# First block's MLP in whole fp32 products, weights split into two parts later, and the second block's attention spread over it

## Chip, cores and metric

One core of one Trainium2 chip runs the kernel once. The metric is the device time of that execution in microseconds, here called us.

## What is computed

The reference chains three layers over 4 x 768 = 3072 tokens of width 384:

```python
# 1. linear attention, 8 heads of 48, a gate f per step and channel
f = 1 / (1 + exp(-f_logit))
for t in range(S):
    state = f[:, :, t, :, None] * state + k[:, :, t] (x) v[:, :, t]
    y[:, :, t] = q[:, :, t] @ state
# 2. MLP, 384 -> 2048 -> 384
h = x @ w_in
g = h * clip(h + 3, 0, 6) / 6
x = g @ w_out
# 3. eight experts, 384 -> 1024 -> 384, one expert for a token
e = argmax(x @ w_gate)
out = prob[e] * sigmoid(x @ w_output_gate)[e] * (relu(x @ w1[e]) @ w2[e])
```

## The kernel before

The tokens go in 8 blocks of 384 (`NB`, `TB`). For each block there are four attention units (`attention`, a pair of heads each, `pr` 0 to 3), then the MLP (`mlp`), then the choice of an expert (`choose`, `route`). After the last block the experts run one after the other.

An attention unit gives VectorE (DVE in the profile) two scans, four products, two masks and a few small sums; ScalarE (ACT) its gates and copies; TensorE (PE) a transpose `pk`, and the products `pa`, `pkv` and `py`, all in plain fp32. Its result `py` is copied out as two parts, an upper one in the reduced format fp32r (by ACT) and a lower one, the rest (by DVE, `L301`). Both parts stand in the tile `xx`. Unit 3 writes them to `yx`, and six DMAs on SyncE's queue (SP, `L305`) then move them to their rows of `xx`, which the MLP waits for.

The MLP goes over 16 slices `f` of 128 hidden columns. In each slice it makes `ph` from three tiles of `w_in` and 384 tokens ("up"), applies `relu6`, and two slices later (`LAG`) adds the slice's part to three accumulators ("down"). Two buffers hold `ph`, so that slice f+2 can begin only when `relu6` has read slice f. Each of the six products of a slice is made of three fp32r products (`mm3`, and `L323` to `L325`): upper times upper, upper times lower, lower times upper. Weights therefore stand in four tiles, `wih`, `wil`, `woh`, `wol`.

The first MLP's weights arrive as raw 64-bit words. `split64` loads 512 columns (`raw`, two buffers, so that a load waits until the one before the last has been read), joins them to fp32 with three instructions of DVE (`L138`, `L140`, `L144`) and one of ACT (`L143`), and splits them with one of ACT (`L145`, upper part) and one of DVE (`L146`, lower part). There are 24 such parts; 7 of them are asked for between the attention units of block 0, the others two for each slice of block 0's MLP.

`UNITS` gives the slices of the MLP at which the attention units of later blocks are written: unit 0 of a block goes two blocks ahead at slice 11, the others at slices 0, 5 and 9 of the block ahead. Unit 0 of block 1 stands ahead of block 0's MLP. In block 0 eight pairs of fill writes (`fill`, `L479`, `L481`, to `xs_d` in DRAM) follow the last weight load on SP.

The order on each engine is made by a scheduler with a timeline of its own when the program is built. Every engine then works through its list strictly in order. The line numbers are those of the profile.

Of the kernel before, what the change touches and what calls it, by code (L numbers as in the profile page):

```python
# [838 lines left out]
```

## Time and profile before

| | |
|---|---|
| time, three runs | 868.16, 870.57, 870.67 us (median 870.57) |
| the profiled execution | 870.31 us, of which the profile's span is 868.6 us |
| busy, of the span | PE 808.3 us (93%), DVE 528.4 us (61%), ACT 398.1 us (46%) |
| PE's clock | 0.963 of full speed, mean over the span |

The profile divides the span into stretches and tells for each engine how long it was busy. PE's granted clock is 1.00 at 2.4 GHz and 0.50 at 1.2 GHz. A matmul's record is longer than its share of the stream, since matmuls overlap: the step from one start to the next tells what it costs. The same holds for DVE.

### The profile page before, as it was taken

How to read it: one execution, taken by the hardware profiler on the slowest of the kernel's cores; microseconds unless marked ns; L12 is line 12 of the kernel's file. 1: busy time of each engine (PE TensorE's matmuls, PEld its weight loads, DVE VectorE, ACT ScalarE, POOL GpSimd, SP SyncE). 2: the span in 40 equal slices, each digit the busy share in tenths (PEclk: the TensorE clock that was granted, in tenths of full speed). 3: DMA queues.
4: the chain of work that ended last, by engine and by line, in shares of the span. 5: the costliest groups of instructions: out<-in, count | busy, mean ns of one | idle time of the engine just before them, and what ended most of it. 6: DMA issues, size and time to landing. Idle time of an engine off the chain costs nothing.

```text
span 868.6 us, 14585 instructions
## 1 busy us (share of the span) xinstructions
PE 808.3 (93%) x5530; PEld 748.6 (86%) x5530; DVE 528.4 (61%) x1122; ACT 398.1 (46%) x848; POOL 61.1 (7%) x103
## 2 busy tenths in 40 slices
PE   7458998999998999999999999999999999999994
PEld 3338998998998998998899899899998999999994
DVE  6999975669555578653668744563465354465441
ACT  4556664446434456533446433453253253354321
POOL 2000000100000010010010010010100101101111
PEclk9558999999999999999999999999999999999998
DMA  6565495113012022111111100050345055246510
GB/s 190 177 186 154 153 288 159 39 57 105 9 62 73 17 70 80 42 61 43 48 62 58 40 29 10 20 167 20 119 126 189 25 181 169 88 149 200 168 53 28
DMA packets 42411, 85.01 MB, mean 98 GB/s; under 512 B 5953, under 2 KB 29794, under 8 KB 42332
## 3 DMA queue, kind: packets, MB, share of 16 engines
q1 hardware_dynamic: 39052, 74.50, 28.5%
q0 software_dynamic: 3280, 9.49, 3.0%
q8 instruction: 45, 0.74, 0.4%
q14 instruction: 34, 0.28, 0.1%
HBM read 65.77 MB, written 16.26 MB: 94 GB/s over the span
## 4 chain that ended last, share of the span: by engine, by line
PE 46%; DVE 5%; DMA 4%; ACT 2%; issue 2%; SPq 0%; POOL 0%; POOLq 0%; DVEq 0%; ACTq 0%
PE ph L310 7%; PE ph L312 7%; PE ph L311 7%; PE yacc L311 4%; PE yacc L312 3%; PE acc L323 3%; PE acc L324 3%; PE acc L325 3%; PE yacc L310 3%; DMA raw<-in_w 3%; PE py L591 1%; PE py L291 1%; PE pa L253 1%; PE px L553 1%; DVE w1l L124 1%
## 5 line engine op out<-in xcount | busy, mean ns | idle before, releaser
L310 PE MATMUL ph<-xx,wih 128*128 128x384 f32 x384 | 133.7, 348 | 9.5 <-DMA xx<-yx 6.3
L312 PE MATMUL ph<-xx,wil 128*128 128x384 f32 x384 | 132.9, 346 | 0.0
L311 PE MATMUL ph<-xx,wih 128*128 128x384 f32 x384 | 131.9, 343 | 0.0
L347 ACT ACTIVATE gf<-ph,three 128x384 f32<-128x384 f32 x128 | 73.7, 580 | 125.4 <-PE ph L312 123.3
L323 PE MATMUL acc<-woh,gh 128*128 128x384 f32 x384 | 129.4, 337 | 0.7 <-ACT gh L349 0.7
L324 PE MATMUL acc<-wol,gh 128*128 128x384 f32 x384 | 129.8, 338 | 0.0
L325 PE MATMUL acc<-woh,gl 128*128 128x384 f32 x384 | 122.0, 337 | 0.0
L348 DVE SCALAR_TENSOR_TENSOR gf<-gf,ph 128x384 f32<-128x384 f32 x128 | 70.4, 553 | 80.0 <-ACT gf L347 79.3
L354 DVE SCALAR_TENSOR_TENSOR hl<-ph,hh 128x256 fp32r<-128x256 f32 (+7 forms) x72 | 39.0, 543 | 88.9 <-ACT hh L353 84.0
L350 DVE TENSOR_TENSOR gl<-gf,gh 128x384 fp32r<-128x384 f32 x128 | 70.8, 555 | 34.8 <-ACT gh L349 33.6
L349 ACT CAST gh<-gf 128x384 fp32r<-128x384 f32 x128 | 65.3, 512 | 52.2 <-DVE gf L348 50.7
L353 ACT ACTIVATE hh<-ph 128x256 fp32r<-128x256 f32 (+7 forms) x72 | 34.5, 480 | 115.6 <-PE ph L312 110.2
L310 PEld LDWEIGHTS ph<-xx,wih 128*128 128x128 f32 x384 | 74.0, 193 | 13.0 <-DMA xx<-yx 7.2
L312 PEld LDWEIGHTS ph<-xx,wil 128*128 128x128 f32 x384 | 73.9, 192 | 0.9 <-issue 0.5
L311 PE MATMUL yacc<-hl,w2h 128*128 128x256 f32 (+7 forms) x216 | 71.8, 339 | 3.1 <-DVE hl L354 3.1
L311 PEld LDWEIGHTS ph<-xx,wih 128*128 128x128 f32 x384 | 73.9, 192 | 0.3
L323 PEld LDWEIGHTS acc<-woh,gh 128*128 128x128 f32 x384 | 72.1, 188 | 1.5 <-ACT gh L349 1.0
L324 PEld LDWEIGHTS acc<-wol,gh 128*128 128x128 f32 x384 | 72.1, 188 | 1.1 <-issue 0.7
L325 PEld LDWEIGHTS acc<-woh,gl 128*128 128x128 f32 x384 | 71.2, 188 | 0.8 <-issue 0.3
L310 PE MATMUL ph<-xh,w1h 128*128 128x256 f32 (+7 forms) x216 | 71.9, 334 | 0.0
L311 PE MATMUL ph<-xl,w1h 128*128 128x256 f32 (+7 forms) x216 | 71.7, 332 | 0.0
L312 PE MATMUL ph<-xh,w1l 128*128 128x256 f32 (+7 forms) x216 | 71.6, 332 | 0.0
(161 smaller groups left out, 1434.9 us busy)
## 6 DMA issues: line engine op xcount, KB each, us to landing
raw<-in_w SPq DMA_DIRECT2D x23, 512.0 KB, 6.1
raw<-in_w SPq DMA_DIRECT2D x30, 384.0 KB, 3.4
vs<-in_v SPq DMA_DIRECT2D x32, 192.0 KB, 2.5
raw<-in_w_in SPq DMA_DIRECT2D x12, 512.0 KB, 4.0
raw<-in_w_out SPq DMA_DIRECT2D x12, 512.0 KB, 3.5
xt<-in_fl SPq DMA_DIRECT2D x32, 168.0 KB, 3.1
kt<-in_k SPq DMA_DIRECT2D x32, 168.0 KB, 2.4
qt<-in_q SPq DMA_DIRECT2D x32, 168.0 KB, 2.5
```

The source lines that it names most:

```text
L310: nc.tensor.matmul(ps, lhsT=wh, rhs=xh, start=first, stop=False)
L311: nc.tensor.matmul(ps, lhsT=wh, rhs=xl, start=False, stop=False)
L312: nc.tensor.matmul(ps, lhsT=wl, rhs=xh, start=False, stop=last)
L323: nc.tensor.matmul(acc[t], lhsT=gh[:, ts_], rhs=w2h[:, f, :], start=f == 0, stop=False)
L324: nc.tensor.matmul(acc[t], lhsT=gh[:, ts_], rhs=w2l[:, f, :], start=False, stop=False)
L325: nc.tensor.matmul(acc[t], lhsT=gl[:, ts_], rhs=w2h[:, f, :], start=False, stop=f == nf - 1)
L347: nc.scalar.activation(gf, ph, AF.Relu, bias=three)
L348: nc.vector.scalar_tensor_tensor(out=gf, in0=gf, scalar=6.0, in1=ph, op0=ALU.min, op1=ALU.mult)
L349: nc.scalar.copy(gh, gf)
L350: nc.vector.tensor_tensor(out=gl, in0=gf, in1=gh.bitcast(F32), op=ALU.subtract)
L353: return (nc.scalar.activation(gh, ph, AF.Relu).ins, nc.vector.scalar_tensor_tensor(out=gl, in0=ph, scalar=0.0, in1=gh.bitcast(F32), op0=A ...
L354: nc.vector.scalar_tensor_tensor(out=gl, in0=ph, scalar=0.0, in1=gh.bitcast(F32), op0=ALU.max, op1=ALU.subtract).ins)
```

## The change

Block 0's MLP takes whole fp32 weights, whole fp32 activations (`x0`, one plane and not two), and one plain fp32 product in place of three fp32r products. `narrow` only joins the words. The tiles of `w_in` keep 512 columns (12 parts), those of `w_out` get 384 (16 parts and not 12). `halve` makes the two parts of a weight for block 1 and later; it is written at slice 11 of block 0 and at the start, slice 2 and slice 6 of block 1. A lower part takes the place of the whole weight before it (`place`), so that its writing waits until block 0 has read that. `relu6` of block 0 writes whole values, and its upper copy and lower subtraction fall away, as do those of the attention result. The units of block 1 are written at slices 0, 4, 8 and 11 of block 0; those of block 2 at the start and slices 2, 5 and 9 of block 1.

```diff
@@ -126,42 +126,63 @@
     SW = 1024
     loads = []
-    def split64(pool, hi, lo, src):
-
-        raw = work.tile([P, SW // 2, 2], U32, tag="raw", name="raw64")
+    def narrow(pool, t, src):
+
+        n = t.shape[1]
+        raw = work.tile([P, SW // 2, 2], U32, tag="raw", name="raw64")[:, 0:n]
         loads.append(nc.sync.dma_start(out=raw.rearrange("p n t -> p (n t)"), in_=src))
         lw, hw = raw[:, :, 0], raw[:, :, 1]
-        s = pool.tile([P, SW // 2], U32, tag="s64", name="s64", bufs=2)
-        t = s.bitcast(I32)
-        r = pool.tile([P, SW // 2], I32, tag="r64", name="r64")
+        r = pool.tile([P, SW // 2], I32, tag="r64", name="r64")[:, 0:n]
+        s = t.bitcast(U32)
         nc.vector.tensor_scalar(out=s, in0=hw, scalar1=3, scalar2=0x3FFFFFFF, op0=ALU.logical_shift_left,
                                 op1=ALU.bitwise_and)
-        nc.vector.scalar_tensor_tensor(out=t.bitcast(U32), in0=hw, scalar=0xC0000000, in1=s, op0=ALU.bitwise_and,
+        nc.vector.scalar_tensor_tensor(out=s, in0=hw, scalar=0xC0000000, in1=s, op0=ALU.bitwise_and,
                                        op1=ALU.bitwise_or)
         nc.scalar.activation(r, lw, AF.Copy, scale=2.0 ** -29)
-        nc.vector.tensor_tensor(out=t, in0=t, in1=r, op=ALU.add)
-        nc.scalar.copy(hi, t.bitcast(F32))
-        nc.vector.tensor_tensor(out=lo, in0=t.bitcast(F32), in1=hi.bitcast(F32), op=ALU.subtract)
-
-    def first_weights(pool):
-        return [pool.tile(sh, F32R, name=n) for n, sh in (("wih", [P, KD, FF]), ("wil", [P, KD, FF]),
-                                                          ("woh", [P, NF, DM]), ("wol", [P, NF, DM]))]
-
-    def load_first(pool, i, wih, wil, woh, wol):
-
-        wohf, wolf = (t.rearrange("p f d -> p (f d)") for t in (woh, wol))
-
-        def up(kt):
-            sl = slice(i * 512, (i + 1) * 512)
-            split64(pool, wih[:, kt, sl], wil[:, kt, sl], w_in.bitcast(U32)[:, kt, 1024 * i:1024 * (i + 1)])
-
-        def down(j):
-            sl = slice(j * 512, (j + 1) * 512)
-            split64(pool, wohf[:, sl], wolf[:, sl], w_out.bitcast(U32)[:, 1024 * j:1024 * (j + 1)])
-
-        return [partial(up, kt) for kt in range(KD)] + [partial(down, j) for j in range(3 * i, 3 * i + 3)]
+        nc.vector.tensor_tensor(out=t.bitcast(I32), in0=t.bitcast(I32), in1=r, op=ALU.add)
+
+    class FirstWeights:
+
+
+
+        def __init__(self, pool, temp):
+            self.pool, self.temp = pool, temp
+            self.hi = [pool.tile(sh, F32R, name=n) for n, sh in (("wih", [P, NF // 4, KD, 512]), ("woh", [P, NF, DM]))]
+            self.whole, self.lo = ({}, {}), ({}, {})
+
+        def place(self, k, j, dt):
+            return (self.temp if j == (KD * NF // 4, NF)[k] else self.pool).tile([P, (512, DM)[k]], dt, tag=f"{'io'[k]}{j}", name=f"{'io'[k]}{j}")
+
+        def load(self, k, j):
+            t = self.whole[k][j] = self.place(k, j + 1, F32)
+            i, kt = divmod(j, KD)
+            narrow(self.temp, t, w_in.bitcast(U32)[:, kt, 1024 * i:1024 * (i + 1)] if k == 0 else
+                   w_out.bitcast(U32)[:, 2 * DM * j:2 * DM * (j + 1)])
+
+        def halve(self, k, j):
+            t = self.whole[k].pop(j)
+            hi = self.hi[0].rearrange("p i k c -> p (i k) c")[:, j, :] if k == 0 else self.hi[1][:, j, :]
+            self.lo[k][j] = self.place(k, j, F32R)
+            split(hi, self.lo[k][j], t, nc.vector)
+
+        def parts(self, do, i):
+
+            return [partial(do, 0, 3 * i + kt) for kt in range(KD)] + [partial(do, 1, f) for f in range(4 * i, 4 * i + 4)]
+
+        def up(self, kt, f):
+            i, c = f // 4, slice(f % 4 * P, f % 4 * P + P)
+            j = KD * i + kt
+            return (None, self.whole[0][j][:, c]) if j in self.whole[0] else (self.hi[0][:, i, kt, c], self.lo[0][j][:, c])
+
+        def down(self, f):
+            return (None, self.whole[1][f]) if f in self.whole[1] else (self.hi[1][:, f, :], self.lo[1][f])
+
...
-        nc.scalar.copy(yx[:, 0, :], py)
-        freed[1:] = [nc.vector.tensor_tensor(out=yx[:, 1, :], in0=py, in1=yx[:, 0, :].bitcast(F32), op=ALU.subtract)]
+        hl = xx.shape[1]
+        yx = xx[:, :, pr, :] if pr < 3 else at1.tile([P, hl, TB], xx.dtype, tag="yx", name="yx")
+        freed[1:] = [nc.scalar.copy(yx[:, 0, :], py)]
+        if hl == 2:
+            freed[1:] = [nc.vector.tensor_tensor(out=yx[:, 1, :], in0=py, in1=yx[:, 0, :].bitcast(F32),
+                                                 op=ALU.subtract)]
...
         def second(f):
-            gh, gl = gs.pop(f)
+            g, (wh, wl) = gs.pop(f), w.down(f)
             for t in range(3):
                 ts_ = slice(t * P, (t + 1) * P)
-                nc.tensor.matmul(acc[t], lhsT=gh[:, ts_], rhs=w2h[:, f, :], start=f == 0, stop=False)
-                nc.tensor.matmul(acc[t], lhsT=gh[:, ts_], rhs=w2l[:, f, :], start=False, stop=False)
-                nc.tensor.matmul(acc[t], lhsT=gl[:, ts_], rhs=w2h[:, f, :], start=False, stop=f == nf - 1)
+                if wh is None:
+                    nc.tensor.matmul(acc[t], lhsT=g[0][:, ts_], rhs=wl, start=f == 0, stop=f == nf - 1)
+                    continue
+                gh, gl = g
+                nc.tensor.matmul(acc[t], lhsT=gh[:, ts_], rhs=wh, start=f == 0, stop=False)
+                nc.tensor.matmul(acc[t], lhsT=gh[:, ts_], rhs=wl, start=False, stop=False)
+                nc.tensor.matmul(acc[t], lhsT=gl[:, ts_], rhs=wh, start=False, stop=f == nf - 1)
...
+                wh, wl = w.up(kt, f)
+                if wh is None:
+                    nc.tensor.matmul(ph, lhsT=wl, rhs=x[0][:, kt, :], start=kt == 0, stop=kt == KD - 1)
+                else:
+                    mm3(ph, wh, wl, x[0][:, kt, :], x[1][:, kt, :], kt == 0, kt == KD - 1)
+            gs[f] = [pool.tile([P, TB], x[0].dtype, tag=n, name=n, bufs=3) for n in ("gh", "gl")[:len(x)]]
+            act(pool, ph, *gs[f])
...
-    def relu6(pool, ph, gh, gl):
+    def relu6(pool, ph, gh, gl=None):
         gf = pool.tile([P, TB], F32, tag="gf", name="gf")
         nc.scalar.activation(gf, ph, AF.Relu, bias=three)
-        nc.vector.scalar_tensor_tensor(out=gf, in0=gf, scalar=6.0, in1=ph, op0=ALU.min, op1=ALU.mult)
-        nc.scalar.copy(gh, gf)
-        nc.vector.tensor_tensor(out=gl, in0=gf, in1=gh.bitcast(F32), op=ALU.subtract)
+        nc.vector.scalar_tensor_tensor(out=gh if gl is None else gf, in0=gf, scalar=6.0, in1=ph, op0=ALU.min, op1=ALU.mult)
+        if gl is not None:
+            nc.scalar.copy(gh, gf)
+            nc.vector.tensor_tensor(out=gl, in0=gf, in1=gh.bitcast(F32), op=ALU.subtract)
...
-            xts[blk] = blkp.tile([P, 2, KD, TB], F32R, tag="xx", name="xx")
+
+            xts[blk] = blkp.tile([P, 1, KD, TB], F32, tag="xx", name="x0") if blk == 0 else blkp.tile(
+                [P, 2, KD, TB], F32R, tag="xx", name="xx")
         attention(blk, pr, xts[blk])
-    wfirst = first_weights(m1)
+    wfirst = FirstWeights(m1, cv)
     UNITS = (-5, 0, 5, 9)
-    parts = [part for i in range(NF // 4) for part in load_first(cv, i, *wfirst)]
-    for pr, n in enumerate((0, 3, 3, 1)):
+    starts = {(blk - 1, f) if f >= 0 else (blk - 2, f + NF): (blk, pr) for blk in range(3, NB) for pr, f in enumerate(UNITS)}
+    starts.update({(0, f): (1, pr) for pr, f in enumerate((0, 4, 8, 11))})
+    starts.update({(1, f): (2, pr) for pr, f in enumerate((-1, 2, 5, 9))})
+    halves = dict(zip(((0, 11), (1, -1), (1, 2), (1, 6)), range(4)))
+    parts = [part for i in range(NF // 4) for part in wfirst.parts(wfirst.load, i)]
+    for pr, n in enumerate((0, 3, 3, 2)):
         att_unit(0, pr)
         with tc.issue_after(ready[-1]):
             for _ in range(n):
                 parts.pop(0)()
-    for pr in range(4):
-        if UNITS[pr] < -1:
-            att_unit(1, pr)
...
+            for part in wfirst.parts(wfirst.halve, halves[blk, f]) if (blk, f) in halves else ():
+                part()
             if blk == 0 and f >= NF - E:
                 with tc.issue_after(loads[-1].ins):
                     fill(f - NF + E)
-            for pr in range(4):
-                if f == UNITS[pr] and blk + 1 < NB:
-                    att_unit(blk + 1, pr)
-                if f == UNITS[pr] + NF and blk + 2 < NB:
-                    att_unit(blk + 2, pr)
+            if (blk, f) in starts:
+                att_unit(*starts[blk, f])
         between(-1)
         xx = xts.pop(blk)
-        acc = mlp(blkp, xx[:, 0], xx[:, 1], *wfirst, NF, relu6, between)
+        acc = mlp(blkp, [xx[:, i] for i in range(xx.shape[1])], wfirst, NF, relu6, between)
```

The scheduler makes of it the following. On DVE, early in the program (unit 1 of block 0 and the first three weight parts), these rows stand before:

```order
L140 SCALAR_TENSOR_TENSOR s64_325<-raw64_323,s64_325 128x512
L235 SCALAR_TENSOR_TENSOR r0_353<-xt_345,rmax_155 112x384
L144 ISA s64_315<-s64_315,r64_316 128x1024
L238 TENSOR_TENSOR kt_344<-kt_344,r0_353 112x384
L146 TENSOR_TENSOR wil_163<-s64_315,wih_162 128x512
L260 TENSOR_TENSOR at_270<-pa1_272,nmask_100 128x384
L144 ISA s64_325<-s64_325,r64_326 128x1024
L260 TENSOR_TENSOR at_270<-pa0_271,nmask_100 128x384
L138 TENSOR_SCALAR s64_335<-raw64_333 128x512
```

and these now:

```order
L140 SCALAR_TENSOR_TENSOR i2_317<-raw64_318,i2_317 128x512
L256 SCALAR_TENSOR_TENSOR r0_343<-xt_335,rmax_155 112x384
L144 ISA i1_309<-i1_309,r64_312 128x1024
L259 TENSOR_TENSOR kt_334<-kt_334,r0_343 112x384
L144 ISA i2_317<-i2_317,r64_320 128x1024
L138 TENSOR_SCALAR i3_325<-raw64_326 128x512
L124 TENSOR_TENSOR i0_1021<-i1_309,wih_162 128x512
L281 TENSOR_TENSOR at_267<-pa1_269,nmask_100 128x384
L281 TENSOR_TENSOR at_267<-pa0_268,nmask_100 128x384
```

The first reading of the third weight part (`L138`) now stands ahead of the unit's two masks (`L260`, now `L281`); one lower part (`L124`) is made here, and the others wait.

On DVE, up to the first `relu6` of block 0's MLP, these rows stand before:

```order
L260 TENSOR_TENSOR at_567<-pa0_568,nmask_100 128x384
L240 SCALAR_TENSOR_TENSOR kb_668<-rg_665,kt_649 112x384
L235 SCALAR_TENSOR_TENSOR r0_944<-xt_936,rmax_155 112x384
L281 TENSOR_TENSOR st_220<-st_220,pkv_578 112x48
L140 SCALAR_TENSOR_TENSOR s64_788<-raw64_786,s64_788 128x512
L146 TENSOR_TENSOR wol_165<-s64_778,woh_164 128x512
L242 TENSOR_TENSOR qt_934<-qt_934,gg_943 112x384
L237 TENSOR_TENSOR rg_951<-r0_944,gg_943 112x384
L238 TENSOR_TENSOR kt_935<-kt_935,r0_944 112x384
L281 TENSOR_TENSOR st_220<-st_220,pkv_578 112x48
L144 ISA s64_788<-s64_788,r64_789 128x1024
L138 TENSOR_SCALAR s64_824<-raw64_822 128x512
L348 SCALAR_TENSOR_TENSOR gf_623<-gf_623,ph_611 128x384
```

and these now:

```order
L144 ISA o8_666<-o8_666,r64_669 128x768
L302 TENSOR_TENSOR st_218<-st_218,pkv_599 112x48
L254 SCALAR_TENSOR_TENSOR gg_1053<-th_1052,zero_154 112x384
L261 SCALAR_TENSOR_TENSOR kb_923<-rg_920,kt_904 112x384
L256 SCALAR_TENSOR_TENSOR r0_1054<-xt_1046,rmax_155 112x384
L140 SCALAR_TENSOR_TENSOR i7_685<-raw64_686,i7_685 128x512
L138 TENSOR_SCALAR i8_693<-raw64_694 128x512
L258 TENSOR_TENSOR rg_1061<-r0_1054,gg_1053 112x384
L259 TENSOR_TENSOR kt_1045<-kt_1045,r0_1054 112x384
L377 SCALAR_TENSOR_TENSOR gh_537<-gf_538,ph_533 128x384
```

The first `relu6` (`L348`, now `L377`) is the 128th row of DVE before and the 124th now; the scans and products of block 1's units 1 to 3 (`gg`, `r0`, `kb`, `kt`, `rg`) have moved ahead of it.

On PE, at the start of block 0's MLP, these rows stand before (`ph_713` and `ph_750` are slices 1 and 2, `py_587` is block 1's unit 0, `pk_672` its unit 1):

```order
L311 MATMUL ph_713<-xx_166,wih_162 128x384
L312 MATMUL ph_713<-xx_166,wil_163 128x384
L291 MATMUL py_587<-at_567,vs_540 64x128 x2
L294 MATMUL py_587<-qt_537,sbd0_158 64x128 x2
L291 MATMUL py_587<-at_567,vs_540 64x128 x2
L294 MATMUL py_587<-qt_537,sbd0_158 64x128 x2
L291 MATMUL py_587<-at_567,vs_540 64x128 x2
L294 MATMUL py_587<-qt_537,sbd0_158 64x128 x2
L248 MATMUL pk_672<-ident_95,kb_668 128x112 x3
L310 MATMUL ph_750<-xx_166,wih_162 128x384
L311 MATMUL ph_750<-xx_166,wih_162 128x384
L312 MATMUL ph_750<-xx_166,wil_163 128x384
```

and these now (`ph_533`, `ph_623`, `ph_647` are slices 0, 1 and 2, `py_608` is block 1's unit 0, `pk_752` its unit 1, `gh_537` what the first `relu6` writes):

```order
L361 MATMUL ph_533<-x0_164,i3_325 128x384
L361 MATMUL ph_623<-x0_164,i3_325 128x384
L312 MATMUL py_608<-at_588,vs_561 64x128 x4
L315 MATMUL py_608<-qt_558,sbd0_158 64x128 x2
L312 MATMUL py_608<-at_588,vs_561 64x128 x2
L315 MATMUL py_608<-qt_558,sbd0_158 64x128 x2
L269 MATMUL pk_752<-ident_95,kb_748 128x112 x3
L361 MATMUL ph_647<-x0_164,i1_309 128x384
L361 MATMUL ph_647<-x0_164,i2_317 128x384
L361 MATMUL ph_647<-x0_164,i3_325 128x384
L348 MATMUL acc0_530<-o1_405,gh_537 128x384
```

Slice 2 takes the buffer of slice 0 and so waits for the first `relu6`, as it did before; one row (`L361`) now stands where three did (`L310` to `L312`).

## Rows read from the trace of the kernel before

**Rows 1.** Busy by stretch: length, PE, PEld, DVE, ACT, POOL us, PE's clock, DMA.

```profile
40.00:60.00 20.00, 11.02 (x72) 7.71 (x73) 18.72 (x40) 11.77 (x27) 0.00 (x0) 0.50 0.59 179
```

**Rows 2.** Timeline of PE: start us, us, line, op, out<-in, shapes, count, [idle before, releaser].

```profile
65.09 0.66 PE L310 MATMUL ph<-xx,wih 128*128 128x384 f32 x1 [0.75 <-DMA xx<-yx]
75.93 0.67 PE L310 MATMUL ph<-xx,wih 128*128 128x384 f32 x1
```

**Rows 3.** Busy time in block 0 from slice 2 on, and in block 1.

```profile
75.90:135.90 60.00, 59.49 (x439) 55.96 (x440) 54.66 (x113) 36.45 (x78) 0.00 (x0) 0.99 0.70 218
...
145.66:208.50 62.84, 62.84 (x466) 58.91 (x466) 45.67 (x103) 32.96 (x78) 3.51 (x5) 1.00 0.19 55
```

**Rows 4.** Timeline of DVE between the first scan of unit 1 and the first relu6.

```profile
14.85 0.96 DVE L233 TENSOR_TENSOR_SCAN gg<-th,zero 112x384 f32<-112x384 f32 x1
...
60.85 0.67 DVE L144 CUSTOM_DVE_ANT_0 s<-s,r 128x1024 uint16<-128x1024 uint16 x1
61.44 0.56 DVE L301 TENSOR_TENSOR yx<-py,yx 128x384 fp32r<-128x384 f32 x1
61.91 0.95 DVE L235 TENSOR_TENSOR_SCAN r<-xt,rmax 112x384 f32<-112x384 f32 x1
62.77 0.67 DVE L140 SCALAR_TENSOR_TENSOR s<-raw,s 128x512 uint32<-128x512 uint32 x1
63.35 0.56 DVE L242 TENSOR_TENSOR qt<-qt,gg 112x384 f32<-112x384 f32 x1
...
72.83 0.43 DVE L138 TENSOR_SCALAR s<-raw 128x512 uint32<-128x512 uint32 x1
73.16 0.56 DVE L348 SCALAR_TENSOR_TENSOR gf<-gf,ph 128x384 f32<-128x384 f32 x1
```

**Rows 5.** Timeline of SP: the issue of the third weight load.

```profile
19.11 0.37 SPq L132 DMA_DIRECT2D raw<-in_w_in  x1
```

**Rows 6.** Timeline of DVE: two readings of weight words that waited for their load.

```profile
24.36 0.43 DVE L138 TENSOR_SCALAR s<-raw 128x512 uint32<-128x512 uint32 x1 [0.18 <-DMA raw<-in_w_in]
...
50.14 0.43 DVE L138 TENSOR_SCALAR s<-raw 128x512 uint32<-128x512 uint32 x1 [1.17 <-DMA raw<-in_w_in]
```

**Rows 7.** Timeline of PE: a `pk`; two records of one plain fp32 product, twice (`keep_warm`).

```profile
8.76 0.48 PE L248 MATMUL pk<-ident,kb 112*128 112x112 f32 x3 [1.47 <-DVE kb L240]
...
9.07 0.50 PE L69 MATMUL warm<-kb,pad 112*128 112x384 f32 x1
...
9.41 0.49 PE L69 MATMUL warm<-kb,pad 112*128 112x384 f32 x1
...
31.04 0.87 PE L69 MATMUL warm<-kb,pad 112*128 112x384 f32 x1
...
31.71 0.85 PE L69 MATMUL warm<-kb,pad 112*128 112x384 f32 x1
```

**Rows 8.** Timeline of PE: three split products and the next.

```profile
79.09 0.33 PE L310 MATMUL ph<-xx,wih 128*128 128x384 f32 x1
...
79.61 0.33 PE L310 MATMUL ph<-xx,wih 128*128 128x384 f32 x1
```

**Rows 9.** Timeline of PE: unit 0 of block 2, and from block 0 to block 1.

```profile
130.98 0.94 PE L253 MATMUL pa<-qt,kb 48*128 48x128 f32 x12
...
132.33 0.44 PE L325 MATMUL acc<-woh,gl 128*128 128x384 f32 x1
...
135.83 0.66 PE L291 MATMUL py<-at,vs 128*64 128x128 f32 x8
...
137.08 0.87 PE L366 MATMUL px<-ident,row 128*128 128x128 f32 x6
140.40 0.41 PE L310 MATMUL ph<-xx,wih 128*128 128x384 f32 x1 [2.44 <-DMA xx<-yx]
...
145.66 0.44 PE L310 MATMUL ph<-xx,wih 128*128 128x384 f32 x1
```

**Rows 10.** Timeline of SP: the block's six DMAs behind the fill writes.

```profile
114.99 0.43 SPq L479 DMA_DIRECT2D xs_d<-pad  x1
...
134.07 5.61 SPq L305 DMA_DIRECT2D xx<-yx  x6
```

More of the change, by code (lines that the diff above doesn't have):

```diff
@@ L166, in second_weights, with __init__ @@
+    class SecondWeights:
+        def __init__(self, w1h, w1l, w2h, w2l):
+            self.up = lambda kt, f: tuple(w[:, kt, f * P:(f + 1) * P] for w in (w1h, w1l))
+            self.down = lambda f: (w2h[:, f, :], w2l[:, f, :])
     def second_weights(pool):
@@ L297, in attention @@
         in_turn(products)
-        yx = xx[:, :, pr, :] if pr < 3 else at1.tile([P, 2, TB], F32R, tag="yx", name="yx")
-        nc.scalar.copy(yx[:, 0, :], py)
-        freed[1:] = [nc.vector.tensor_tensor(out=yx[:, 1, :], in0=py, in1=yx[:, 0, :].bitcast(F32), op=ALU.subtract)]
+        hl = xx.shape[1]
[4 more added lines that the diff above has]
+                                                 op=ALU.subtract)]
         if pr == 3:
@@ L312, in mm3, with mlp @@
         nc.tensor.matmul(ps, lhsT=wl, rhs=xh, start=False, stop=last)
-    def mlp(pool, xth, xtl, w1h, w1l, w2h, w2l, nf, act, between=None):
+    def mlp(pool, x, w, nf, act, between=None):
         acc = [ps_acc.tile([P, DM], F32, tag=f"acc{t}", name=f"acc{t}") for t in range(3)]
@@ L329, in mlp @@
             ph = ps_h.tile([P, CAP], F32, tag="h", name="ph")[:, 0:TB]
-            fs = slice(f * P, (f + 1) * P)
             for kt in range(KD):
-                mm3(ph, w1h[:, kt, fs], w1l[:, kt, fs], xth[:, kt, :], xtl[:, kt, :], kt == 0, kt == KD - 1)
-            gh = pool.tile([P, TB], F32R, tag="gh", name="gh", bufs=3)
-            gl = pool.tile([P, TB], F32R, tag="gl", name="gl", bufs=3)
-            act(pool, ph, gh, gl)
-            gs[f] = (gh, gl)
+                wh, wl = w.up(kt, f)
[5 more added lines that the diff above has]
+            act(pool, ph, *gs[f])
             if f >= LAG:
@@ L729, in fused @@
             gp = es.enter_context(tc.tile_pool(name="gw", bufs=1))
-            wg1 = first_weights(gp)
-            for i in range(NF // 4):
-                for part in load_first(gp, i, *wg1):
-                    part()
+            wg1 = FirstWeights(gp, gp)
+            for do in (wg1.load, wg1.halve):
+                for i in range(NF // 4):
+                    for part in wg1.parts(do, i):
+                        part()
             with tc.For_i(0, NB, 1) as nb:
@@ L750, in keep @@
                     nc.sync.dma_start(out=x2_d[bass.ds(nb, 1)].rearrange("a p k t -> p (a k) t"), in_=x2)
-                row, oh = choose(gp, mlp(gp, xth, xtl, *wg1, NF, relu6), keep)
+                row, oh = choose(gp, mlp(gp, (xth, xtl), wg1, NF, relu6), keep)
                 gs = gp.tile([P, E, 3, 2], F32, tag="gs", name="gs")
@@ L780, in fused @@
                     nc.sync.dma_start(out=yo, in_=yo_d[bass.ds(nb, 1)].rearrange("a p t d -> p (a t) d"))
-                    acc = mlp(gp, xth, xtl, *w2s, NFE, relu)
+                    acc = mlp(gp, (xth, xtl), SecondWeights(*w2s), NFE, relu)
                     for t in range(3):
```

## The prediction

> **What bounds the kernel now.** I read the table of stretches first. From 40 to 60 us DVE is busy 18.72 of 20 us and PE 11.02, at a granted clock of 0.50 [rows 1]: until block 0's MLP gets going, the kernel waits for DVE. From 75.90 to 135.90 PE is busy 59.49 of 60.00 us, and in block 1, from 145.66 to 208.50, all of 62.84 [rows 3]: from there a microsecond more of PE's work is a microsecond more of time, and any free time of DVE is worth nothing.
>
> The point where the one limit hands over to the other stands in two timelines. PE's slices 0 and 1 begin at 65.09, when `xx` has landed, but slice 2 begins only at 75.93 [rows 2]: it needs the buffer of slice 0, so the first `relu6`, and that stands on DVE at 73.16 behind weight parts and attention [rows 4]. I call this `relu6` the turn. The last place is the step from block 0 to block 1: the last product of block 0 ends at 135.9 (the end of the first stretch of [rows 3]), unit 0 of block 2 has its `py` after it, and block 1's first product comes at 140.40 after 2.44 us of idle waiting for `xx`. Its third slice begins at 145.66 [rows 9]. The six DMAs were issued at 134.07, behind fill writes that had begun at 114.99 [rows 10].
>
> **What a product costs.** A split product is three records and steps 0.52 us (79.09 to 79.61 [rows 8]). A plain fp32 product over 384 columns is two records with 0.34 from start to start (9.07 to 9.41), or 0.67 each later, from 31.04 to 31.71 [rows 7]. At full clock I take 0.667 for the product: 0.147 more than split. The change has fewer records and costs PE more. The 90 products from slice 2 of block 0 on (14 slices up, 16 down, three each) cost 60.0 instead of 46.8 us, +13.2. The six of slices 0 and 1 lie before the turn. The rows are given to 0.01, so the bounds are 0.65 and 0.68 (two steps of 0.34): 58.5 and 61.2.
>
> The Trainium skill speaks against the change more strongly: "FP8 and Floating Point Precision", section "TensorE Precision Notes", gives true FP32 four passes through the array. By four passes at a third of 0.52 each, a product would cost 0.693 us (an estimate from that page and the row above), the 90 products 62.4 us, and the end would come 2.4 us later than I forecast. The step in the trace is near this and I go by the step.
>
> **DVE up to the turn.** From the first scan at 14.85 to the turn at 73.16 [rows 4] DVE passes 58.3 us with 111 rows of its list. In the new list:
> - lower halves of weights (`L146`): 12 go, 2 `L124` come. The neighbours of 512 columns step 0.59 (60.85 to 61.44) and 0.58 (62.77 to 63.35) [rows 4]; ten at 0.6 are -6.0;
> - four lower halves of the attention result (`L301`, 0.47 from 61.44 to 61.91 [rows 4]): -1.9;
> - joining: 14 `L138`, 13 `L140`, 13 `L144` of 512 columns become 16, 15 and 14, of which about half have 384. With 0.33 for `L138` (72.83 to 73.16), 0.6 for the others [rows 4] and 384 in proportion: -0.2;
> - two scans (0.86, 61.91 to 62.77 [rows 4]) and three products at 0.47 of block 1's units come ahead of the turn: +3.1.
>
> The net is -5.0 us of work. Waits come against it. The first reading of the third load now stands two rows after the second part's last step, ahead of the masks. That load was issued at 19.11 [rows 5], its reading in the old order was at 24.36 and had to wait 0.18, and another load cost 1.17 at 50.14 [rows 6]. By my sum DVE gets to the third reading at 21.5, so it waits 2.75 for a landing at 24.3. Behind that `L138` stand the masks of unit 1 and all the rest. I add 1.1 for one more like that of 50.14 and 0.65 for a `w_out` part: 4.5 us of stalls. Before there were 2.6 in all: 1.35 for these two loads and the rest small waits for PE and ACT, for which the longer stand at the load leaves time. Turn: 73.16 - 5.0 + 1.9 = 70.1. With no stalls at all it is 65.6, with 7 us of them 72.6.
>
> Can `x0` be later than that? Before, 3.1 us passed from the end of `L301` (61.44 + 0.56 [rows 4]) to 65.09. The lower half is gone and the list ahead is shorter, so I expect the first product at 58 to 60. Slices 0 and 1 take 4.0 us, or 8.0 at the longer step of [rows 7]: done by 68. If nothing came earlier, it would be 69 to 73. So DVE keeps the turn. The scans and products that moved ahead are also why slice 2 need not wait longer than the `relu6` (before, unit 1's `pk` stood between and waited for its `kb` on DVE, behind the `relu6`): slice 2 begins at 70.5, against 75.93.
>
> **Block 0 from slice 2.** Of PE's 59.49 us [rows 3], 46.8 were products, so 12.7 attention. Unit 0 of block 2 leaves: `pa` and `pkv` from 130.98 to 132.33, 1.35 [rows 9], `pk` 0.31 (8.76 to 9.07 [rows 7]). That leaves 11.0. Last down product: 70.5 + 60.0 + 11.0 = 141.5, 5.6 later. DVE was busy 54.66 us here [rows 3]. It loses 16 lower subtractions of `relu6` (16 at 0.47, 7.5 us) and the rest of 24 `L146`, and gets 26 `L124`, each of which waits until block 0 has read the place that it writes. Going through both new lists row by row with these prices, DVE stays ahead until slice 8 and then waits for PE, never the other way; this cover is some 3 to 6 us.
>
> **The step to block 1.** The last `py` of unit 3 now stands three products before block 0's end (2 us), and its six DMAs come after it, at about 140, when the fills (ended by 134 before, and not moved later) are gone from SP. From `py` to a landed `xx` I take 4 us, 3.1 for the transfer as above and the copies: 1.9 us of wait after the last product, in which `px` runs. Then 18 records up to the third slice at 0.173 (a third of 0.52), 3.1, where before they took 5.26 (140.40 to 145.66 [rows 9]), and 0.8 for a `relu6` that stands on DVE behind the choice's small steps: the third slice at 147.3. Unit 0 of block 2 now costs block 1 its 1.35 + 1.25 (`py`, 135.83 to 137.08 [rows 9]) + 0.31 = 2.9 us on a PE with no free time [rows 3]. All told 147.3 + 2.9 = 150.2 against 145.66: +4.5. All 28 lower parts are made by then. Blocks 2 to 7 and the experts are unchanged and bound by PE, so this shift stays.
>
> **Sum.** The profiled execution took 870.31 us, 0.26 under the median of 870.57. 870.3 + 4.5 = 874.8. What a measurement can tell from no change is 0.3%, 2.6 us.
>
> **Rivals.**
> - *Faster.* DVE's stalls vanish, since the third load is there in time (it waits only as long as before), and the turn comes at 65.6 or sooner with `x0` at 58. Then slice 2 begins 4.5 us earlier than I say. With a step to block 1 that waits nothing (another 1.9) it ends at 868.4; with a product at 0.65 at 866.9. By the turn alone it is 870.3, no gain. It decides from a turn before 66 with that step free, or before 63 without. For: a reading waited 0.18 only [rows 6]. Against: that was at 24.36, and the new order asks 3 us sooner. 0.11.
> - *No change.* The turn at 67 to 68, or the step to block 1 without a wait, each 2 to 3 us less than my sum: 868 to 873, about 871.5. 0.21.
> - *DVE late.* 384-wide parts cost as much as 512 (16 parts, 3 steps, and 12 `L124`, up to 8 us more), or lower parts hold a `relu6` in the first eight slices. The cover of 3 to 6 us is used up: some 3 us more, 876 to 879. 0.18.
> - *The clock.* After waits at the turn or at the step to block 1, PE's products take the longer step of [rows 7]. Six of them at 1.33 instead of 0.667 are 4 us, and the 18 records as before 2.2: 877 to 881. 0.10.
> - *Nothing like it*: a plain product as cheap as one record (0.17), as the fewer rows suggest. Then it would be 34 us faster (96 times 0.35); [rows 7] exclude it.
>
> **Numbers.** My forecast, 873 to 877, has 0.40. Slower by over 0.3% is all from 873.2 up: 0.40 + 0.18 + 0.10, so 0.68; same 0.21; faster 0.11. From 868 to 880 leaves out the best half of the faster case and the worst of the clock, 1 in 10 together; the likeliest case's own is 873 to 877.
>
> **What would show it.** The first `relu6` (now `L377`) near 70, with a wait for `raw` of 2 to 3 us at the third `L138`; `L361` records at steps of 0.33; block 0's last product at 141; the six DMAs after the fills and under 2.5 us of idle before block 1's first product; no wait of PE for `relu6` from slice 3 on; and the shift at block 1's end kept to the end. It is wrong if the turn is under 67 or over 72, if products step under 0.31 or over 0.35 a record, or if PE waits for DVE inside block 0.

## The result, and the profile after

The changed kernel takes 881.28 us (median of 4 runs, 878.62 to 883.72) against 870.30 us before (4 runs): a ratio of 1.0128, 95% interval 1.0104 to 1.0152. It is slower by 11 us; 4.5 were forecast, and the time lies 1.3 us above the range. The profiled execution has a span of 879.2 us against 868.6, so 10.6 us are to be found in the traces.

The first place is DVE ahead of the first `relu6`. These are the rows of the changed kernel's DVE timeline that wait for a load, and the first `relu6` (start us, us, engine, line, operation, names, shapes, count, idle before and what ended it):

```profile
25.44 0.43 DVE L138 TENSOR_SCALAR i<-raw 128x512 uint32<-128x512 uint32 x1 [3.17 <-DMA raw<-in_w_in]
...
37.96 0.36 DVE L138 TENSOR_SCALAR o<-raw 128x384 uint32<-128x384 uint32 x1 [1.52 <-DMA raw<-in_w_out]
...
49.90 0.43 DVE L138 TENSOR_SCALAR i<-raw 128x512 uint32<-128x512 uint32 x1 [1.77 <-DMA raw<-in_w_in]
...
54.65 0.36 DVE L138 TENSOR_SCALAR o<-raw 128x384 uint32<-128x384 uint32 x1 [0.90 <-DMA raw<-in_w_out]
...
74.92 0.55 DVE L377 SCALAR_TENSOR_TENSOR gh<-gf,ph 128x384 f32<-128x384 f32 x1
```

The reader is to see four waits of 7.36 us together where there were two of 1.35 [rows 6], and a first `relu6` at 74.92, later than the 73.16 of [rows 4], though DVE has less to do. The gaps in the list from the first scan (15.02, against 14.85 before) to that `relu6` add up to 8.59 us, against 2.55 in the same stretch before; the work in between shrank from 55.8 to 51.3.

The second place is PE from there to block 1. Rows of its timeline, the same columns:

```profile
65.06 5.60 PE L361 MATMUL ph<-x,i 128*128 128x384 f32 x12 [2.12 <-DMA x<-yx]
...
75.53 2.20 PE L361 MATMUL ph<-x,i 128*128 128x384 f32 x6 [1.00 <-DVE gh L377]
77.57 2.10 PE L348 MATMUL acc<-o,gh 128*128 128x384 f32 x6
79.50 2.10 PE L361 MATMUL ph<-x,i 128*128 128x384 f32 x6
81.44 2.10 PE L348 MATMUL acc<-o,gh 128*128 128x384 f32 x6
...
144.16 1.29 PE L396 MATMUL px<-ident,row 128*128 128x128 f32 x9
146.37 0.41 PE L334 MATMUL ph<-xx,wih 128*128 128x384 f32 x1 [0.93 <-DMA xx<-yx]
...
147.52 0.69 PE L404 MATMUL pl<-xTh,wgs 128*32 128x384 f32 x3
148.04 0.69 PE L404 MATMUL pl<-xTl,wgs 128*32 128x384 f32 x3
148.56 0.34 PE L334 MATMUL ph<-xx,wih 128*128 128x384 f32 x1
...
150.75 0.37 PE L412 MATMUL pt<-ident,lgT 32*128 32x32 f32 x3
151.93 0.44 PE L334 MATMUL ph<-xx,wih 128*128 128x384 f32 x1 [0.81 <-DVE gf L377]
```

Slice 2 waits for the first `relu6`, at 75.53, where it began at 75.93 before [rows 2]: the head start that was to pay for the change is 0.4 us. Three products step 1.93 us (77.57 to 79.50), 0.643 each. Block 1's third slice comes at 151.93, 6.3 us later than in [rows 9].

By stretches (length, then busy us and instructions of PE, PEld, DVE, ACT, POOL; PE's clock, DMA share, GB/s), block 0 from slice 2 to its end, to be held against the first line of [rows 3]:

```profile
75.53:144.16 68.63, 68.63 (x319) 41.56 (x320) 51.42 (x106) 29.12 (x61) 0.00 (x0) 1.00 0.65 200
```

PE never rests, at full clock, 8.6 us longer than before, and DVE has 17 us to spare. Set end to end, the 10.6 us are: slice 2 0.4 sooner, block 0 8.6 longer, the step to block 1 2.0 shorter, block 1 up to its `px` (the first records behind its last product, 221.66 against 212.04) 3.4 longer, and 1.0 behind that.

### The profile page after: what moved, and what is told of

It is laid out like the page before. It is cut to its first block, busy times and chain, and to the rows that moved or that the text cites. A ratio compares the mean times of both kernels' runs of the same rounds, so it can differ in the third digit from the quotient of the medians.

```text
span 879.2 us, 14394 instructions
## 1 busy us (share of the span) xinstructions
PE 816.1 (93%) x5434; PEld 730.4 (83%) x5434; DVE 522.1 (59%) x1118; ACT 391.9 (45%) x840; POOL 59.1 (7%) x103
## 4 chain that ended last, share of the span: by engine, by line
PE 75%; DMA 10%; DVE 8%; ACT 3%; issue 3%; SPq 1%; POOL 0%; POOLq 0%; DVEq 0%; ACTq 0%
PE ph L334 10%; PE ph L336 10%; PE ph L335 9%; PE acc L353 6%; PE acc L352 6%; PE acc L351 6%; PE yacc L335 3%; PE acc L348 3%; PE yacc L336 3%; PE ph L361 3%; PE yacc L334 3%; PE py L312 3%; PE pa L274 2%; PE py L315 2%; DMA raw<-in_w 2%
## 5 line engine op out<-in xcount | busy, mean ns | idle before, releaser
L334 PE MATMUL ph<-xx,wih 128*128 128x384 f32 x336 | 115.5, 344 | 9.5 <-DMA xx<-yx 7.8
L352 PE MATMUL acc<-o,gh 128*128 128x384 f32 x336 | 114.2, 340 | 0.0
L351 PE MATMUL acc<-woh,gh 128*128 128x384 f32 x336 | 113.6, 338 | 0.6 <-ACT gh L379 0.6
L336 PE MATMUL ph<-xx,i 128*128 128x384 f32 x336 | 114.0, 339 | 0.0
L335 PE MATMUL ph<-xx,wih 128*128 128x384 f32 x336 | 113.4, 338 | 0.0
L353 PE MATMUL acc<-woh,gl 128*128 128x384 f32 x336 | 107.3, 337 | 0.0
L377 DVE SCALAR_TENSOR_TENSOR gf<-gf,ph 128x384 f32<-128x384 f32 x112 | 61.4, 551 | 72.7 <-ACT gf L376 72.5
L334 PEld LDWEIGHTS ph<-xx,wih 128*128 128x128 f32 x336 | 63.5, 189 | 12.2 <-DMA xx<-yx 9.3
L336 PE MATMUL yacc<-hh,w2l 128*128 128x256 f32 (+7 forms) x216 | 70.8, 334 | 0.0
L336 PEld LDWEIGHTS ph<-xx,i 128*128 128x128 f32 x336 | 63.4, 189 | 1.5 <-issue 1.4
L335 PEld LDWEIGHTS ph<-xx,wih 128*128 128x128 f32 x336 | 63.6, 189 | 0.2
L352 PEld LDWEIGHTS acc<-o,gh 128*128 128x128 f32 x336 | 63.1, 188 | 0.6 <-issue 0.2
```

Source lines behind the costliest of these rows:

```text
L334: nc.tensor.matmul(ps, lhsT=wh, rhs=xh, start=first, stop=False)
L335: nc.tensor.matmul(ps, lhsT=wh, rhs=xl, start=False, stop=False)
L336: nc.tensor.matmul(ps, lhsT=wl, rhs=xh, start=False, stop=last)
L351: nc.tensor.matmul(acc[t], lhsT=gh[:, ts_], rhs=wh, start=f == 0, stop=False)
L352: nc.tensor.matmul(acc[t], lhsT=gh[:, ts_], rhs=wl, start=False, stop=False)
L353: nc.tensor.matmul(acc[t], lhsT=gl[:, ts_], rhs=wh, start=False, stop=f == nf - 1)
```

## Experiments

Each time is the median of its runs; ratios are to the kernel before on the same chip in the same session. Turn means the first `relu6` on DVE, as in the prediction.

**1. Four raw buffers.** The place of block 1's attention result, not yet in use, holds two more.

```diff
+    more = blkp.tile([P, 2, KD, TB], F32R, tag="xx", name="more").rearrange("p h k t -> p h (k t)").bitcast(U32)
+    wfirst.more = [more[:, h, 0:SW].rearrange("p (n t) -> p n t", t=2) for h in range(2)]
...
+            m = len(loads)
+            raw = self.more[m // 2 % 2] if self.more and m in (1, 3, 5, 7) else None
```

> The changed kernel with four buffers for the raw words of the first eight weight loads in place of two (two of them lie in the place of block 1's attention result, which nothing uses yet). Theory A: the changed kernel's DVE waits 7.4 us for loads ahead of the first relu6 because each load must wait for the reading of the load before the last. Then the waits at the third, sixth, eighth and tenth reading shrink to under 2 us together, the first relu6 comes at 69 to 70 in place of 74.9, and the end follows it by about 5 us: 875 to 877 against 881. Rival B: the loads are late by themselves (DMA engines busy, 3.3 to 5.2 us from issue to landing); the waits stay and the time stays 881. Rival C: the first relu6 comes earlier, but the end doesn't follow, since PE then waits for DVE later in block 0: 879 to 881.

875.92 us, 1.0070 (1.0052 to 1.0087). The end is where theory A put it, the turn is not (69 to 70 expected). The gaps ahead of the turn were 6.58 us against 8.59 and the turn came at 72.88; run 9 shows that single traces of one kernel differ nearly as much, so that only the time of this run says that the buffers helped. The second load now was the late one: SP issued the first and the third at 4.57 and 5.04, the second only at 18.06, and its reading waited 2.04 us. So it isn't the number of buffers alone; a load also has its place in SP's queue.

**2 and 3. The spread of the units.** Alone on the kernel before, and taken back in the changed one.

```diff
+    starts.update({(0, f): (1, pr) for pr, f in enumerate((0, 4, 8, 11))})
+    starts.update({(1, f): (2, pr) for pr, f in enumerate((-1, 2, 5, 9))})
...
-            for pr in range(4):
-                if f == UNITS[pr] and blk + 1 < NB:
-                    att_unit(blk + 1, pr)
...
+            if (blk, f) in starts:
+                att_unit(*starts[blk, f])
```

> The kernel before with the new slices for the attention units alone; split products and split weights as before. Theory A: the spread alone moves 2.9 us of PE's work from block 0 to block 1 and shortens the wait between the two; about the time of before, 868 to 872. Rival B: the spread carries a part of the loss (attention ahead of the first relu6 on DVE): 874 to 876.

> The changed kernel with the attention units at the slices of before; whole fp32 products kept. Theory A: the products' price and the late first relu6 are the loss, so it stays: 879 to 884. Rival B (the spread is the loss): 873 to 876.

871.78 us, 1.0021 (1.0002 to 1.0040), and 879.25 us, 1.0109 (1.0090 to 1.0128). The spread moves unit 0 of block 2 from block 0 to block 1: in run 2 block 0 ends at 134.1, block 1's third slice starts at 145.94, about as before, and from there to block 1's `px` it takes 68.1 us against 66.4. Both times point the same way, to a cost of the spread of some 1.5 to 2 us, at the edge of what can be told from nothing. The rest of the loss stays with the whole products and what belongs to them. So do the waits for loads: ahead of the turn DVE waited 0.84 us for them in run 2 and 6.64 in run 3.

**4. The price of a product.** This run leaves out a fifth of the columns of block 0's product.

```diff
+                    c = DM if f == 0 else 304
+                    nc.tensor.matmul(acc[t][:, 0:c], lhsT=g[0][:, ts_], rhs=wl[:, 0:c], start=f == 0, stop=f == nf - 1)
...
+                    c = TB if kt == 0 else 272
+                    nc.tensor.matmul(ph[:, 0:c], lhsT=wl, rhs=x[0][:, kt, 0:c], start=kt == 0, stop=kt == KD - 1)
```

> The changed kernel, with block 0's plain products cut to 384, 272 and 272 columns in each up product of three and to 304 in the down products behind the first slice, so that each costs PE about what a split product did (0.52 us). It leaves out a fifth of block 0's product, nothing else changes. Theory A: from slice 2 on PE sets the pace, so 90 products cheaper by 0.13 us give 11 to 12 us back: 869 to 870, about the time of before. Rival B: DVE sets the pace in block 0 as well, it then waits for nothing and the gain is under 4 us: 877 or more.

869.24 us, 0.9996 (0.9983 to 1.0010): theory A. With products at about the price of split ones (three up products step 1.56 us, 80.21 to 81.77) the whole loss is gone, so PE sets the pace of block 0: from slice 2 to its `px` it takes 57.9 us in place of 68.6. It shows the other half too. DVE had been relieved here as well, and the kernel is no faster than before: its turn is at 74.34, with 7.56 us of gaps ahead of it, and slice 2 begins at 75.89, where it began at 75.93 before. The relief was worth nothing.

**5. No waits for loads.** This run leaves out nine loads; the parts are joined from the words of the first two.

```diff
+        if not 2 <= count[0] < 11:
+            held[:] = held[-1:] + [work.tile([P, SW // 2, 2], U32, tag="raw", name="raw64")]
...
+        raw = held[count[0] % 2][:, 0:n] if 2 <= count[0] < 11 else held[-1][:, 0:n]
```

> The changed kernel, in which the third to the eleventh weight part are joined from the words of the first two loads, so that nine loads are left out (and those weights are wrong values); all instructions of DVE, ACT and PE stay. Theory A: the waits for loads (7.4 us) are the whole reason for the late first relu6, and block 0 follows it one to one. Then the first relu6 comes at 66 to 68 in place of 74.9 and the end at 873 to 875. Rival B: something else holds the first relu6 as well (the landing of x0, at 65.1, ends the first two slices at 70.7): it comes at 71 to 72 and the end is 877 to 878. Rival C: the end does not follow: 880 or more.

873.20 us, 1.0032 (1.0016 to 1.0048), theory A as to the turn and the end; "one to one" did not hold. The turn is at 67.89, with 1.11 us of gaps ahead of it, and slice 2 begins at 68.50, 7.0 us sooner. It is given back in part at once: PE had waited 3.04 us before it, and from 70 to 75 us its granted clock is 0.58, against 1.00 in the changed kernel, so that slice 3 begins at 75.28, only 4.2 us sooner. PE's timeline there, and the stretch (columns as above):

```profile
68.50 4.21 PE L366 MATMUL ph<-x,i 128*128 128x384 f32 x6 [3.04 <-DVE gh L382]
...
70.00:75.00 5.00, 5.00 (x11) 2.72 (x10) 4.70 (x10) 1.82 (x5) 0.00 (x0) 0.58 0.42 133
```

**6. Four raw buffers, another order.** As run 1, but with `raw = self.more[m % 2] if self.more and m in (2, 3, 6, 7) else None`.

> As the run with four raw buffers, but with the first two loads in the old buffers and the third, fourth, seventh and eighth in the new ones. In the run before, only one load was issued at the start and the wait moved to the second reading (2.04 us). Theory A (issue order on SP and the buffers together): the third load is now issued at 17.7 to 18.1, behind a load of values that waits for its buffer, and lands at 22.5; its wait falls from 3.17 to about 1 us, the other three to under 1.5 in sum, the first relu6 at 70 to 71.5, the end at 874 to 876. Rival B (loads late by the DMA engines): waits of 5 to 7 us in sum remain, the end 876 to 878, as in the first trial.

874.99 us, 1.0061 (1.0039 to 1.0083): theory A's time, with waits somewhat longer than it said. In DVE's timeline two loads are waited for, and the turn is about where the prediction had put it:

```profile
22.55 0.43 DVE L140 TENSOR_SCALAR i<-more 128x512 uint32<-128x512 uint32 x1 [1.79 <-DMA more<-in_w_in]
...
38.74 0.43 DVE L140 TENSOR_SCALAR i<-raw 128x512 uint32<-128x512 uint32 x1 [1.76 <-DMA raw<-in_w_in]
...
69.82 0.53 DVE L381 SCALAR_TENSOR_TENSOR gh<-gf,ph 128x384 f32<-128x384 f32 x1
```

The gaps ahead of it are 4.79 us (forecast for the changed kernel: 4.5) and the time is 875.0 (forecast: 874.8). That the time agrees so closely is in part luck: here block 0 ends 1.2 us sooner than in the sum (`px` at 140.31, forecast 141.5) and the step to block 1 takes 2.0 more (7.8 for 5.8).

**7. Lower halves on POOL**, in the kernel before: another way to relieve DVE, which costs PE nothing.

```diff
-        nc.vector.tensor_tensor(out=lo, in0=t.bitcast(F32), in1=hi.bitcast(F32), op=ALU.subtract)
+        nc.gpsimd.tensor_tensor(out=lo, in0=t.bitcast(F32), in1=hi.bitcast(F32), op=ALU.subtract)
```

> The kernel before, with the lower halves of the first weights (24 subtractions of 128 x 512) on POOL, which is idle there, in place of DVE. It takes the same 7 us (12 of 0.6) off DVE ahead of the first relu6 that the change took, without plain products. Theory A: the first relu6 comes 5 to 7 us earlier and PE's work in block 0 is the same: 864 to 867 against 870. Rival B: loads then hold DVE as they do in the changed kernel and half of it is lost: 867 to 869. Rival C: POOL and DVE slow each other, or POOL's subtraction takes so long (over 3 us) that lower halves come late: 870 or more.

872.90 us, 1.0030 (1.0010 to 1.0049): rival C. The turn came at 80.87, 7.7 us later than before, with hardly more gaps (2.78 us): DVE's own instructions had become longer, by some 11 us. This is an estimate from the steps of [rows 4]: the work between the first scan and the turn grew by 7.4 us, although 12 subtractions (7.2) had left it, so 14.6 came in; two scans, three products and an `L140` that the new list has ahead of the turn are 3.7 of these, and the rest is length. By block 1's `px` 3.7 us of the delay are left (215.70 against 212.04); why it shrinks stays open. On the longer instructions, see the last section.

**8. Runs 4 and 6 together.**

> Both edits at once: block 0's plain products cut to the price of split ones (a fifth of the product left out), and the second form of the four raw buffers. Theory A (price of PE and waits for loads are two separate losses that add up): -12 from the one and -6 from the other, 862 to 865 against 881 for the changed kernel and 870 for the one before; the relief of DVE is then worth its 5 to 6 us. Rival B: with cheaper products PE waits for DVE or for x0 instead, the gains overlap: 867 or more.

869.30 us, 1.0007 (0.9990 to 1.0024): a time of rival B's range, though not by rival B's way. By the trace, block 0's `px`, which follow its last product, begin at 126.96 against 133.81 in run 4, so up to there the two gains do add up (6.9 us). Then they are lost. PE's timeline of run 8 at the step to block 1:

```profile
126.96 1.29 PE L402 MATMUL px<-ident,row 128*128 128x128 f32 x9
128.89 0.68 PE L410 MATMUL pl<-xTh,wgs 128*32 128x384 f32 x3 [0.64 <-ACT xTh L403]
133.36 0.66 PE L338 MATMUL ph<-xx,wih 128*128 128x384 f32 x1 [3.79 <-DMA xx<-yx]
140.43 0.44 PE L338 MATMUL ph<-xx,wih 128*128 128x384 f32 x1 [0.80 <-DVE gf L383]
```

and SP's timeline there:

```profile
121.59 1.20 SPq L520 DMA_DIRECT2D xs_d<-pad  x1
122.83 1.04 SPq L522 DMA_DIRECT2D xs_d<-pad  x1
...
126.98 5.30 SPq L333 DMA_DIRECT2D xx<-yx  x6
```

The six DMAs were issued behind the last fill writes. From 110 to 130 the DMA engines were fully busy. PE idled 3.79 us, against 0.33 in run 4, and from 130 to 140 its clock was 0.66. It is what [rows 9] and [rows 10] show of the kernel before, whose clock was 0.72 from 140 to 146.

**9. The changed kernel again**, for the spread of sessions.

> The changed kernel once more, unaltered, for a ratio on the same chip and in the same session: 1.010 to 1.015 of the kernel before. If it comes out at 1.006 or less, the differences of the runs with four raw buffers were not from their edit.

879.82 us, 1.0126 (1.0097 to 1.0156), as expected; the turn at 74.68. This second trace of one kernel also tells how far a single trace can be trusted: its first scan comes 1.3 us later than in the first (16.28 against 15.02), its gaps ahead of the turn are 7.0 us and not 8.6, and its span is 1.7 us shorter. The four loads that are waited for are the same. Run 1's gaps (6.58) are close to this scatter, those of runs 5 (1.11) and 6 (4.79) far from it.

**10. Run 8 with the fills early**: between the loads, not behind them.

```diff
-            if blk == 0 and f >= NF - E:
+            if blk == 0 and 4 <= f < 4 + E:
```

> The run with cheap products and four raw buffers, with the eight fill writes at slices 4 to 11 of block 0, between the weight loads, in place of 8 to 15 behind the last of them. In that run block 0 ended 6.9 us sooner than with cheap products alone, and the six DMAs of the attention result were then issued at 127.0 right behind the fills and landed late: 3.8 us of idle PE and a stretch at 0.66 of the clock. Theory A: the fills took the gain back; with them out of the way the first product of block 1 waits under 2 us and the end is 863 to 865. Rival B: the fills slow the weight loads and with them DVE in block 0, or the wait is from something else: 868 or more.

864.08 us, 0.9947 (0.9930 to 0.9963), theory A. At the same place PE now waits 0.19 us, and the third slice of block 1 begins 3.6 us sooner, though block 0 ended 1.8 us later:

```profile
128.79 1.29 PE L402 MATMUL px<-ident,row 128*128 128x128 f32 x9
130.72 0.69 PE L410 MATMUL pl<-xTh,wgs 128*32 128x384 f32 x3 [0.64 <-ACT xTh L403]
131.59 0.41 PE L338 MATMUL ph<-xx,wih 128*128 128x384 f32 x1 [0.19 <-DMA xx<-yx]
136.81 0.45 PE L338 MATMUL ph<-xx,wih 128*128 128x384 f32 x1 [0.80 <-DVE gf L383]
```

From 120 to 134 PE was busy 13.17 us at clock 1.00, against 9.58 at 0.88 in run 8.

**11 and 12. Early fills alone**, in the kernel before and in run 6's.

> The kernel before with the same edit alone. Theory A: its 2.44 us wait for the attention result ahead of block 1 and the slow 18 records behind it (5.26 us in place of 3.1) come from the fills as well: 865 to 867 against 870. Rival B: DVE is busy 55 of 60 us in this block, and loads that come late between fills hold it: 870 or more.

> The changed kernel with four raw buffers (second form) and the early fills. Its block 0 ends at 140, some 10 us after the fills, so theory A says that there is nothing to gain: 874 to 876, as without the early fills. Rival B: fills among the loads cost DVE time in block 0: 877 or more.

869.72 us, 0.9994 (0.9974 to 1.0015), and 876.24 us, 1.0088 (1.0067 to 1.0109). In the kernel before the loss moved: the wait for `xx` is gone, but PE waits for DVE inside block 0, 3.42 us at 126.22 alone. DVE had waited 2.49 us for a weight load at 123.38. That is rival B, at a time 0.3 us under it. Run 12 lies between theory A (up to 876) and rival B (from 877), and its trace shows rival B's mechanism too: a late load holds DVE, and PE waits for DVE inside block 0, which it did nowhere behind slice 2 in run 6.

```profile
114.21 0.36 DVE L140 TENSOR_SCALAR o<-raw 128x384 uint32<-128x384 uint32 x1 [2.62 <-DMA raw<-in_w_out]
...
117.14 3.89 PE L365 MATMUL ph<-x,i 128*128 128x384 f32 x6 [2.08 <-DVE gh L381]
```

So there was nothing to gain, and by its trace moving the fills among the loads cost something: from slice 2 to `px` block 0 took 72.3 us against 69.9 in run 6. The two times, 1.2 us apart, do not tell it from noise.

## Why the prediction was wrong in its size

The direction held, and so did the price of the product on PE. The turn did not: it was forecast 3.1 us sooner than before and came 1.8 later, 4.8 off. None of the rivals had it late for this reason. Against the sum:

**The turn** (70.1 forecast, 74.92 measured; over 72 was one of the prediction's own signs of being wrong). The step that failed is "4.5 us of stalls": it counted the third load (2.75; it was 3.17) and then "1.1 for one more like that of 50.14 and 0.65 for a `w_out` part". There were four waits for loads, 7.36 us, and small ones besides: 8.59. Of the 4.8 us, 4.1 are these stalls, 0.5 are work (DVE's shrank by 4.5 us, for 5.0 forecast) and 0.2 the later first scan.

What it missed shows when the issue of a load is held against the moment at which DVE is ready to read it. SP issued the four loads that were waited for, in the order of reading the third, sixth, ninth and eleventh (run 1's expectation names the third, sixth, eighth and tenth), here:

```profile
18.97 0.37 SPq L133 DMA_DIRECT2D raw<-in_w_in  x1
...
33.06 0.33 SPq L133 DMA_DIRECT2D raw<-in_w_out  x1
...
45.21 0.37 SPq L133 DMA_DIRECT2D raw<-in_w_in  x1
...
51.45 5.18 SPq L133 DMA_DIRECT2D raw<-in_w_out  x3
```

From SP's and DVE's timelines of both kernels, in us after the issue (DVE is ready where its wait begins, or where it reads without one; where no landing is on record, the end of the wait stands for it):

| load | before: DVE ready, landed | changed: DVE ready, landed |
|---|---|---|
| third | 5.1, 5.2 | 3.3, 6.5 |
| sixth | 4.0, 3.6 | 3.4, 4.9 |
| ninth | 4.0, 5.1 | 2.9, 4.7 |
| eleventh | 4.6, 3.5 | 2.3, 3.2 |

A part now has three instructions of DVE and not four, with the same two buffers, and the loads stand in SP's queue behind the attention's. DVE is ready 0.6 to 2.3 us sooner after the issue, and the load's way to landing, 3 to 6 us, is no longer covered by its work. Every part can meet this, not two of them. Run 3 has waits at the same four loads and run 2 only one, of 0.84, so they come with the narrow parts and not with the spread; whether the fewer instructions, the 384-wide parts or the new order weigh most was not tested apart. That the waits make the turn late and the kernel slower is shown by runs 5 and 6: with the waits gone or lessened the turn goes to 67.9 and 69.8 and the time to 873 and 875. The prediction's upper bound, 72.6 with 7 us of stalls, was too tight as well.

**The product** (+13.2 us for 90, from a step of 0.667). The step is 0.643 to 0.647, just under the prediction's bounds, and block 0 from slice 2 took 68.6 us (75.53 to 144.16) where 71.0 were forecast: 2.4 us less. That PE pays for each product is shown by run 4. The step is 0.05 us under the estimate of 0.693 from the Trainium skill's four passes ("FP8 and Floating Point Precision", "TensorE Precision Notes"): the estimate was too high, while how many passes the array makes no run here shows.

**Block 0's DVE.** Right: PE waits for DVE once, at slice 2 (1.00 us), and then not before block 1. DVE is busy 51.42 of 68.63 us with the lower parts among its work, and they hold nobody up.

**The step to block 1** (5.8 us from the last product to the third slice; 7.8 measured, 144.16 to 151.93). The fills were gone and the wait for `xx` short (0.93), as said. Left out were the choice's `pl` records, 1.04 us (147.52 to 148.56), and `pt`, 0.37, which stand among the 18; `px` with the wait behind it took 0.3 more than the 1.9 forecast, and the 18 records 0.2 more than 3.1.

**Unit 0 of block 2 in block 1** (+2.9). Block 1's `px` are 9.6 us later than before, its third slice 6.3: +3.3. From there to the end the shift grows by 1.0 us more. The prediction had it stay as it was; the two traces of the changed kernel differ by 1.7 us in their spans, so that no cause can be named for this 1.0.

Slice 2 +5.0, block 0 -2.4, the step +2.0, block 1 +0.4 and the rest +1.0 make 6.0 more than the 4.5 forecast, 10.5 of the 10.6 in the spans. Of the rivals, the clock and a late DVE in block 0 did not happen here (the clock was 1.00 in block 0 and from 144 to 152); the clock did in runs 5 and 6, where PE had waited 3.04 and 2.78 us and was then granted 0.58 and 0.66 from 70 to 75 us. The prediction split the spread over its terms and gave no price for the whole; runs 2 and 3 put it at some 2 us or less.

## What to carry to other kernels

Work that is taken off a busy engine pays only as far as its inputs come sooner too: count the new distance from a load's issue to its reading against the time from issue to landing, for every load and not for the two that waited before. A product in full fp32 is paid on TensorE (0.645 us here, for 0.52 split), and a stage bound by it returns nothing of what other engines save. When a stage ends sooner, look at what it then runs into, as run 8 ran into the fill writes. Run 10, which like run 8 leaves out a fifth of the product, gained once the fills were moved too; in the kernels of runs 11 and 12 the same move gained nothing.

## What had not been expected of the hardware

POOL's subtractions made DVE's instructions longer. In run 7 DVE's groups up to the turn (count, then busy us and mean ns of one) are these:

```profile
L144 DVE CUSTOM_DVE_ANT_0 s<-s,r 128x1024 uint16<-128x1024 uint16 x13 | 11.6, 892 | 1.4 <-ACT r L143 1.3
...
L235 DVE TENSOR_TENSOR_SCAN r<-xt,rmax 112x384 f32<-112x384 f32 x6 | 7.8, 1292 | 0.0
...
L260 DVE TENSOR_TENSOR at<-pa,nmask 128x384 f32<-128x384 f32 x8 | 4.3, 549 | 0.0
```

Before, `L144` took 685 ns, the scan `L235` 953 and `L260` 551. The longer ones stand beside a subtraction of POOL. Of DVE's timeline in run 7:

```profile
25.37 1.64 DVE L140 SCALAR_TENSOR_TENSOR s<-raw,s 128x512 uint32<-128x512 uint32 x1
...
38.95 1.01 DVE L260 TENSOR_TENSOR at<-pa,nmask 128x384 f32<-128x384 f32 x2
...
41.62 1.90 DVE L233 TENSOR_TENSOR_SCAN gg<-th,zero 112x384 f32<-112x384 f32 x1
```

and of POOL's:

```profile
25.00 1.45 POOL L146 TENSOR_TENSOR wil<-s,wih 128x512 fp32r<-128x512 f32 x1 [1.28 <-ACT wih L145]
...
38.70 1.46 POOL L146 TENSOR_TENSOR wol<-s,woh 128x512 fp32r<-128x512 f32 x1 [1.28 <-ACT woh L145]
41.43 1.28 POOL L146 TENSOR_TENSOR wol<-s,woh 128x512 fp32r<-128x512 f32 x1 [1.28 <-ACT woh L145]
```

An `L140` that takes 0.68 us alone took 1.64, a scan of 0.96 took 1.90: 0.96 and 0.94 us more, a little less than POOL's instruction still had to run when they began (1.08 and 1.09). `L260`, which reads one input from PSUM, stayed as it was beside POOL: the two from 38.95 lie wholly within a subtraction. This agrees with the Trainium skill, "SBUF — State Buffer", section "Who interferes with whom": a DVE instruction with two SBUF inputs and a GpSimd instruction that reads SBUF lock each other out of a shared port.
